# Weight conversion 512 columns at a time, norms' roots by Newton steps on VectorE, and the second attention beside the first part of the first mixing

## The chip, the cores and the metric

The kernel runs on one core of one Trainium2 chip. The metric is the device time of one execution in microseconds (us). Executions of the kernel before agreed within 0.5% on each chip that was used.

## The reference

Inputs are `q`, `k`, `v` of shape (8 batches, 12 heads, 448 rows, 64 columns) in fp32, the gains `g_q` and `g_k`, and four weight matrices that `setup_inputs` makes in float64 (a float32 array times a numpy float64 scalar stays 64-bit here). Cut to what matters:

```python
def rmsnorm(x, g):
    return x / np.sqrt(np.mean(x * x, axis=-1, keepdims=True) + 1e-06) * g
q_n, k_n = rmsnorm(q, g_q), rmsnorm(k, g_k)
attn = softmax(scale * q_n @ k_n^T)                  # per batch and head
x = (attn @ v), heads side by side                   # (8, 448, 768)
h = np.maximum(x^T @ w_tok1, 0) @ w_tok2             # mixing of rows, 448 -> 256 -> 448
u = x + h^T
return u + np.maximum(u @ w_ch1, 0) @ w_ch2          # mixing of columns, 768 -> 1536 -> 768
```

There are eight attentions and eight mixings, one each per batch.

## The kernel before

TensorE does the column mixing as block products with seven products in place of eight, for which its weights are needed as four blocks and four sums of blocks. So each weight tile is a **stage**: 128 partitions, 512 columns in, eight blocks of 128 out. A stage is converted from the two 32-bit halves of each 64-bit number: VectorE masks the exponent and the high mantissa bits, ScalarE turns both into floats, VectorE puts in the low half and the sign, and GpSimd multiplies mantissa by exponent. 36 stages are converted in this way, stored to DRAM, and reloaded for every batch as **units** of 384 KB.

```python
WCOLS = 256                         # a stage is two items of 256 columns

def convert_first(i):               # item i
    nc.vector.tensor_scalar(e_t[0:rows, 0:n], hi, 0x7FF00000, None, ALU.bitwise_and)      # L201
    nc.vector.tensor_scalar(m_t[0:rows, 0:n], hi, 0x000FFFFF, None, ALU.bitwise_and)      # L202

def convert_second(i):              # ScalarE, one item later
    nc.scalar.activation(out=e, in_=e, func=AF.Relu, bias=expo_c[0:rows, 0:1], scale=8.0)
    nc.scalar.activation(out=m.bitcast(F32), in_=m, func=AF.Identity, bias=one_c[0:rows, 0:1], scale=2.0**-20)

def convert_last(i):                # two items later
    nc.vector.scalar_tensor_tensor(out=mf, in0=lo, scalar=2.0**-52, in1=mf, op0=ALU.mult, op1=ALU.add)              # L227
    nc.vector.scalar_tensor_tensor(out=e, in0=hi, scalar=0x80000000, in1=e, op0=ALU.bitwise_and, op1=ALU.bitwise_or) # L229
    nc.gpsimd.tensor_tensor(out=dst, in0=fold(mf), in1=fold(ef), op=ALU.mult)             # L231, "the product"
    if at >= 0 and at % 2 == 1:     # the second half of a stage
        combine(at // 2)

def combine(j):                     # the stage's sums
    nc.vector.tensor_tensor(out=q[:, 4], in0=q[:, 1], in1=q[:, 3], op=ALU.add)            # L178, waits for the product
    nc.vector.tensor_tensor(out=q[:, 6], in0=q[:, 1], in1=q[:, 0], op=ALU.subtract)       # L179
    nc.gpsimd.tensor_tensor(out=q[:, 5], in0=q[:, 4], in1=q[:, 0], op=ALU.subtract)       # L180
    nc.gpsimd.tensor_tensor(out=q[:, 7], in0=q[:, 2], in1=q[:, 5], op=ALU.subtract)       # L181
    nc.sync.dma_start(out=to.rearrange("q p n -> p q n"), in_=q[:])

def one(i):                         # one item, in the order of issue
    convert_first(i); convert_second(i - 1); convert_last(i - 2); weight_load(i + 2)
```

The norm of a pair of heads (ScalarE squares, VectorE adds up, GpSimd takes the power -0.5), and the order of the whole:

```python
nc.vector.tensor_reduce(out=ms[...], in_=sq[...], axis=AX_X, op=ALU.add)                  # L749
nc.vector.tensor_scalar(ms[0:R, w], ms[0:R, w], 1.0 / D, 1e-6, ALU.mult, ALU.add)         # L753, 16 columns
nc.gpsimd.tensor_tensor(out=rs[0:R, w], in0=ms[0:R, w], in1=..., op=ALU.pow)              # L754
...
BEFORE = len(first) + 4 * KC + 3
for _, fn in merge(att_items(0, AHEAD * per + 2), weight_items(0, BEFORE)):               # attention 0
    fn()
for b in range(B):
    early, late = mlp_items(b)       # mixing b: its first part, its second layer
    if b == 0:
        then = len(first) + 2 * stage_end[3] + 2
        early = merge(early, weight_items(BEFORE, then))
        late = merge(late[:14], weight_items(then, len(chunks) + 2)) + late[14:]
    att = att_items(lo, lo + per) if b + AHEAD < B else []      # attention b + 1
    for _, fn in merge(att, early + late):
        fn()
```

## Time and profile before

| | before |
|---|---|
| median, range of 3 runs | 1572.7 us, 1570.44 to 1574.23 |
| TensorE busy over the span | 1422.2 us, 90% |
| first 403.5 us (attentions 0 and 1, all conversions, mixing 0) | "the ramp" below is the part to the last stage's store, 22.0 to 369.6 us |
| each later batch | 174.5 us, TensorE busy for 172.4 |

The prediction, further down, shows the slices, the stretches and VectorE's waits in the ramp. One more view of it will be needed: VectorE's groups of instructions in the ramp, 22.0 to 369.6 us. The columns are line, engine, operation, tiles, shapes and count; then busy us and mean ns of one; then idle time just before them, and what ended it.

```profile
L227 DVE SCALAR_TENSOR_TENSOR m_t<-raw,m_t 128x256 f32<-128x256 uint32 (+1 forms) x80 | 36.8, 460 | 9.1 <-ACT m_t L213 9.1
L229 DVE SCALAR_TENSOR_TENSOR e_t<-raw,e_t 128x256 uint32<-128x256 uint32 (+1 forms) x80 | 35.7, 446 | 0.0
L202 DVE TENSOR_SCALAR m_t<-raw 128x256 uint32<-128x256 uint32 (+1 forms) x78 | 33.5, 429 | 0.0
L201 DVE TENSOR_SCALAR e_t<-raw 128x256 uint32<-128x256 uint32 (+1 forms) x78 | 31.8, 408 | 8.7 <-DMA raw<-in_moe_w_ch_dram 8.7
...
L753 DVE TENSOR_SCALAR ms<-ms 112x16 f32<-112x16 f32 x12 | 15.2, 1268 | 0.4
```

The means are the thing to look at. Left alone, the masks L201 and L202 take 0.28 us and L227 and L229 take 0.41; in the ramp they average 0.41 to 0.46. L753 takes 0.17 left alone and averages 1.27. In order of time one sees who holds them (start, duration, engine, instruction, all in us):

```profile
311.35 1.30 POOL L562 TENSOR_TENSOR hb<-hb 128x448 f32<-128x448 f32 x1
...
311.59 1.34 DVE L229 SCALAR_TENSOR_TENSOR e_t<-raw,e_t 128x256 uint32<-128x256 uint32 x1
312.86 0.28 DVE L201 TENSOR_SCALAR e_t<-raw 128x256 uint32<-128x256 uint32 x1
...
313.01 0.72 POOL L231 TENSOR_TENSOR stage<-m_t,e_t 128x256 f32<-128x256 f32 x1 [0.36 <-DVE e_t L229]
313.06 0.82 DVE L202 TENSOR_SCALAR m_t<-raw 128x256 uint32<-128x256 uint32 x1
```

L229 starts while GpSimd's L562 runs and is not done before it has ended (311.35 + 1.30 = 312.65), at three times its free duration. L202 meets the product of the item before. Such time counts as VectorE's busy time in the page, not as a wait. **Held time** below is worked out so: for each conversion instruction of the ramp that took over 0.06 us more than its free duration, the excess, summed.

### The profile page before, as it was taken

The page shows a single profiled execution, that of the slowest core. Times are in us where ns is not written, and L with a number is a line of the kernel's source. Part 1 is how long each engine was busy: PE and PEld are TensorE (multiplying, and loading weights), DVE is VectorE, ACT ScalarE, POOL GpSimd, SP SyncE. Part 2 cuts the span into 40 slices and gives each one's busy share as a digit, 9 for nine tenths or more (in the row PEclk, how much of TensorE's full clock was granted, in tenths as well). Part 3 has the DMA queues.
Part 4 walks back from the last instruction along what each step waited for, and adds up shares of the span by engine and source line. Part 5 has one row for each costly group of instructions (what it writes and reads, how often), then busy time and mean ns, then how long its engine had stood idle before and what let it go on. Part 6 is the DMA issues. An engine that isn't in the chain of part 4 may idle for free.

```text
span 1571.7 us, 19052 instructions
## 1 busy us (share of the span) xinstructions
PE 1422.2 (90%) x6976; PEld 1054.9 (67%) x6976; DVE 662.5 (42%) x1183; ACT 511.1 (33%) x930; POOL 612.6 (39%) x514
## 2 busy tenths in 40 slices
PE   5765866497999999999999999999999999999997
PEld 2222454375577866887577766788588767787897
DVE  5765866743344233432434234433343225322321
ACT  6553444332333233322333233323333242312110
POOL 5674566644235324333235224352334234320231
PEclk9786997798999999999999999999999999999999
DMA  5456667476244552455244542555254433444353
GB/s 125 117 146 192 185 205 216 145 227 188 79 136 129 155 144 68 145 147 154 61 140 133 161 119 79 156 147 156 54 149 136 149 103 98 136 127 126 111 171 108
DMA packets 229802, 217.10 MB, mean 138 GB/s; under 512 B 98180, under 2 KB 185988, under 8 KB 229700
## 3 DMA queue, kind: packets, MB, share of 16 engines
q1 hardware_dynamic: 206178, 204.55, 44.5%
q10 hardware_dynamic: 23522, 11.24, 2.7%
q8 instruction: 58, 0.95, 0.2%
q14 instruction: 44, 0.36, 0.1%
HBM read 185.86 MB, written 29.88 MB: 137 GB/s over the span
## 4 chain that ended last, share of the span: by engine, by line
PE 76%; DVE 8%; POOL 6%; DMA 3%; issue 3%; ACT 2%; ACTq 1%; SPq 0%; POOLq 0%; DVEq 0%
PE m_ps L581 24%; PE m_ps L523 22%; PE s_ps L289 8%; PE o_ps L346 8%; PE m_ps L445 5%; PE m_ps L453 4%; PE d_ps L360 2%; POOL rs L754 2%; DMA raw<-in_moe_w_ch_dram 2%; POOL stage L231 2%; PE t_ps L424 2%; PE t_ps L274 2%; DVE m_t L202 1%; DVE m_t L227 1%; DVE e_t L229 1%
## 5 line engine op out<-in xcount | busy, mean ns | idle before, releaser
L581 PE MATMUL m_ps<-hb,unit 128*128 128x224 f32 x2016 | 402.0, 357 | 31.4 <-DMA unit<-ws 31.4
L581 PEld LDWEIGHTS m_ps<-hb,unit 128*128 128x128 f32 x2016 | 378.5, 192 | 53.7 <-issue 26.5
L295 ACT ACTIVATE e<-s_ps,rs 112x448 f32<-112x448 f32 x384 | 212.0, 633 | 190.4 <-PE s_ps L289 190.3
L523 PE MATMUL m_ps<-tu,unit 128*128 128x224 f32 x1152 | 232.9, 356 | 4.3 <-DVE r L528 4.3
L523 PEld LDWEIGHTS m_ps<-tu,unit 128*128 128x128 f32 x1152 | 217.6, 192 | 14.8 <-issue 8.5
L289 PE MATMUL s_ps<-qkT 64*112 64x448 f32 x768 | 181.6, 594 | 25.6 <-ACT qkT L276 25.6
L754 POOL TENSOR_TENSOR rs<-ms,mhalf_c 112x16 f32<-112x16 f32 (+1 forms) x49 | 148.6, 3033 | 103.2 <-DVE ms L753 94.3
L523 PE MATMUL m_ps<-uT,unit 128*128 128x224 f32 x864 | 179.4, 360 | 3.3 <-DVE r L528 3.3
L523 PEld LDWEIGHTS m_ps<-uT,unit 128*128 128x128 f32 x864 | 163.5, 193 | 22.6 <-issue 13.7
L346 PE MATMUL o_ps<-e,vt 112*64 112x448 f32 x768 | 170.0, 565 | 2.4 <-DVE uT L378 2.4
L590 POOL TENSOR_TENSOR uT<-uT,r 128x448 f32<-128x448 f32 (+1 forms) x64 | 58.7, 928 | 283.9 <-DVE r L590 168.0
L332 POOL TENSOR_TENSOR es<-e 112x896 f32<-112x896 f32 x48 | 100.1, 2085 | 125.2 <-PE d_ps L360 125.2
L289 PEld LDWEIGHTS s_ps<-qkT 64*112 64x112 f32 x768 | 65.8, 183 | 103.6 <-issue 65.9
L276 ACT ACTIVATE qkT<-t_ps,g_t 128x448 f32<-128x448 f32 x96 | 58.0, 630 | 211.4 <-PE t_ps L274 207.3
L346 PEld LDWEIGHTS o_ps<-e,vt 112*64 112x64 f32 x768 | 47.8, 139 | 117.0 <-issue 101.6
L445 PE MATMUL m_ps<-x,w_sb 112*128 112x384 f32 x256 | 94.2, 519 | 30.2 <-DVE x L430 17.9
L590 DVE TENSOR_TENSOR uT<-uT,m_ps 128x448 f32<-128x448 f32 (+1 forms) x80 | 38.8, 502 | 195.3 <-PE m_ps L581 160.5
L336 DVE TENSOR_TENSOR es<-es,e 112x896 f32<-112x896 f32 x96 | 115.2, 1200 | 11.2 <-ACT e L295 6.6
L372 DVE STREAM_TRANSPOSE dt<-d_ps 128x448 f32<-128x448 f32 x48 | 31.1, 649 | 189.4 <-PE d_ps L360 189.2
L528 DVE TENSOR_TENSOR r<-m_ps,r 128x448 f32<-128x448 f32 x72 | 44.9, 623 | 137.8 <-PE m_ps L523 94.1
L528 POOL TENSOR_TENSOR hb<-r,r 128x448 f32<-128x448 f32 x24 | 29.3, 1221 | 187.3 <-ACT r L544 187.3
L231 POOL TENSOR_TENSOR stage<-m_t,e_t 128x256 f32<-128x256 f32 x72 | 56.0, 779 | 101.2 <-DVE e_t L229 99.0
(65 smaller groups left out, 1379.8 us busy)
## 6 DMA issues: line engine op xcount, KB each, us to landing
unit<-ws SPq DMA_DIRECT2D x336, 384.0 KB, 3.3
raw<-in_moe_w_ch_dram SPq DMA_DIRECT2D x72, 256.0 KB, 3.4
ws<-stage SPq DMA_DIRECT2D x36, 512.0 KB, 3.5
vt<-in_v_dram SPq DMA_DIRECT2D x48, 224.0 KB, 2.6
out_dram<-y ACTq DMA_DIRECT2D x48, 224.0 KB, 3.3
qk<-in_q_dram SPq DMA_DIRECT2D x92, 112.0 KB, 3.5
qk<-in_k_dram SPq DMA_DIRECT2D x92, 112.0 KB, 3.3
raw<-in_moe_w_tok_dram SPq DMA_DIRECT2D x4, 224.0 KB, 3.7
```

What stands on the lines that cost most here:

```text
L231: nc.gpsimd.tensor_tensor(out=dst, in0=fold(mf), in1=fold(ef), op=ALU.mult)
L289: nc.tensor.matmul(out=ps[0:R, 0:S], lhsT=qkT[a * D:(a + 1) * D, 1, kc * R:(kc + 1) * R], rhs=qkT[a * D:(a + 1) * D, 0, :], start=True, st ...
L295: nc.scalar.activation(out=e[0:R, a, i, :], in_=pss[a][0:R, 0:S], func=AF.Exp, scale=st["rs", p][0:R, r:r + 1])
L332: nc.gpsimd.tensor_tensor(out=es[0:R], in0=e[0:R, :, 0, :], in1=e[0:R, :, 1, :], op=ALU.add)
L336: nc.vector.tensor_tensor(out=es[0:R], in0=es[0:R], in1=e[0:R, :, i, :], op=ALU.add)
L346: nc.tensor.matmul(out=o[a * D:(a + 1) * D, 0:S], lhsT=vt[0:R, a, kc * D:(kc + 1) * D], rhs=e[0:R, a, i, :], start=(kc == 0), stop=(kc == ...
L445: nc.tensor.matmul(out=ps[:, 0:HC], lhsT=w1_sb[0:R, c, jc * P:(jc + 1) * P], rhs=st["x", h][0:R, c, :], start=(c == 0), stop=(c == NS - 1))
L523: nc.tensor.matmul(out=ps[:, j * HS:(j + 1) * HS], lhsT=w[:, t, j, :], rhs=m, start=(t == 0), stop=(t == KC - 1))
L528: add = lambda e, o, x, y: e.tensor_tensor(out=o, in0=x, in1=y, op=ALU.add)
L581: nc.tensor.matmul(out=ps[:, j * HS:(j + 1) * HS], lhsT=st["w"](j, t), rhs=hb[:, HB[what], t, :], start=(t == 0), stop=(t == KF - 1))
L590: add = lambda e, o, x, y: e.tensor_tensor(out=o, in0=x, in1=y, op=ALU.add)
L754: nc.gpsimd.tensor_tensor(out=rs[0:R, w], in0=ms[0:R, w], in1=self.mhalf_c[0:R].to_broadcast([R, (hi - lo) * n]), op=ALU.pow)
```

## The change

Three things are changed at once. A stage becomes one item of 512 columns, its conversion four VectorE instructions instead of eight, with the mantissa kept in the raw buffer; fewer buffers pay for the wider tiles. The root is taken on VectorE by a first guess in integers and three Newton steps, ten instructions of 16 columns, so that GpSimd has no power to do. And attention 1 is merged with the first part of mixing 0 only, the second layer following alone; the conversions are spread anew (`BEFORE`). The diff, cut to its core:

```diff
-    UNITS = 7
+    UNITS = 5
-    cv_pool = pool("cv_pool", 4)
+    cv_pool = pool("cv_pool", 3)
-    WCOLS = 256
+    WCOLS = 512
 ...
     def convert_first(i):
-        nc.vector.tensor_scalar(e_t[0:rows, 0:n], hi, 0x7FF00000, None, ALU.bitwise_and)
-        nc.vector.tensor_scalar(m_t[0:rows, 0:n], hi, 0x000FFFFF, None, ALU.bitwise_and)
+        nc.vector.tensor_scalar(e, hi, 0x000FFFFF, 0x00100000, ALU.bitwise_and, ALU.bitwise_or)
+        nc.vector.scalar_tensor_tensor(
+            out=lo.bitcast(F32), in0=lo, scalar=2.0**-32, in1=e, op0=ALU.mult, op1=ALU.add)
+        nc.vector.tensor_scalar(e, hi, 0x7FF00000, None, ALU.bitwise_and)
 ...
     def convert_second(i):
         nc.scalar.activation(out=e, in_=e, func=AF.Relu, bias=expo_c[0:rows, 0:1], scale=8.0)
-        nc.scalar.activation(
-            out=m.bitcast(F32), in_=m, func=AF.Identity, bias=one_c[0:rows, 0:1], scale=2.0**-20)
+        m = st["raw", i][0:rows, 0:n, 0].bitcast(F32)
+        nc.scalar.mul(m, m, 2.0**-20)
 ...
     def convert_last(i):
-            nc.vector.scalar_tensor_tensor(
-                out=mf, in0=lo, scalar=2.0**-52, in1=mf, op0=ALU.mult, op1=ALU.add)
             nc.vector.scalar_tensor_tensor(
                 out=e, in0=hi, scalar=0x80000000, in1=e, op0=ALU.bitwise_and, op1=ALU.bitwise_or)
-            nc.gpsimd.tensor_tensor(out=dst, in0=fold(mf), in1=fold(ef), op=ALU.mult)
-        at = i - len(first)
-        if at >= 0 and at % 2 == 1:
-            combine(at // 2)
+            nc.gpsimd.tensor_tensor(out=dst, in0=fold(lo.bitcast(F32)), in1=fold(e.bitcast(F32)), op=ALU.mult)
+        if i >= len(first):
+            combine(i - len(first))
 ...
-    BEFORE = len(first) + 4 * KC + 3
+    BEFORE = len(first) + 4
-            then = len(first) + 2 * stage_end[3] + 2
+            then = len(first) + stage_end[3] + 2
-        for _, fn in merge(att, early + late):
+        for _, fn in merge(att, early) + late if b == 0 else merge(att, early + late):
 ...
-            nc.gpsimd.tensor_tensor(
-                out=rs[0:R, w], in0=ms[0:R, w],
-                in1=self.mhalf_c[0:R].to_broadcast([R, (hi - lo) * n]), op=ALU.pow)
+            self.rsqrt(rs[0:R, w], ms[0:R, w])
+
+    def rsqrt(self, y, x):
+        t = self.st_pool.tile([128, 4 * self.NS], F32, name="nt")[0:y.shape[0], 0:y.shape[1]]
+        nc.vector.tensor_scalar(
+            y.bitcast(I32), x.bitcast(I32), -0.5, float(0x5F3759DF), ALU.mult, ALU.add)
+        for _ in range(3):
+            nc.vector.scalar_tensor_tensor(out=t, in0=y, scalar=-0.5, in1=y, op0=ALU.mult, op1=ALU.mult)
+            nc.vector.tensor_tensor(out=t, in0=t, in1=x, op=ALU.mult)
+            nc.vector.scalar_tensor_tensor(out=y, in0=t, scalar=1.5, in1=y, op0=ALU.add, op1=ALU.mult)
```

More of the change, by code (lines that the diff above doesn't have):

```diff
@@ L119, in weight_chunks @@
         w1v = moe_w_tok1.rearrange("(p c) n -> p c n", c=NS)
-        for c in range(NS):
-            for o in range(0, DT, WCOLS):
-                n = min(WCOLS, DT - o)
-                first.append((R, w1v[:, c, o:o + n], w1_sb[0:R, c, o:o + n], None))
+        for c in range(0, NS, 2):
+            first.append((R, [w1v[:, c:c + 2, :].rearrange("p c n -> p (c n)")], w1_sb[0:R, c:c + 2, :].rearrange("p c n -> p (c n)"), None))
         for j in range(NJ):
-            for o in range(0, S, WCOLS):
-                n = min(WCOLS, S - o)
-                dst = w2_sb[:, j, :, o // NS:(o + n) // NS].rearrange("p c r -> p r c")
-                first.append((P, moe_w_tok2[j * P:(j + 1) * P, o:o + n], dst, NS))
+            dst = w2_sb[:, j].rearrange("p c r -> p r c")
+            first.append((P, [moe_w_tok2[j * P:(j + 1) * P, :]], dst, NS))
         for w, group, m, t in stages:
-            rows, cols = (DC if w is moe_w_ch2 else C) // 2, w.shape[1] // 2
-            for k in range(2):
-                r = k * rows + t * P
-                src = w[r:r + P].rearrange("p (i n) -> p i n", i=2)[:, :, m * P:(m + 1) * P]
-                second.append((P, src, None, None))
+            rows = (DC if w is moe_w_ch2 else C) // 2
+            src = [w[r:r + P].rearrange("p (i n) -> p i n", i=2)[:, :, m * P:(m + 1) * P]
+                   for r in (t * P, rows + t * P)]
+            second.append((P, src, None, None))
         return first, second
@@ L143, in stage_list, with columns @@
         return l
+    def columns(i):
+        return WCOLS if chunks[i][2] is None else chunks[i][1][0].shape[-1]
     def weight_load(i):
-        rows, src, dst, split = chunks[i]
-        n = WCOLS if dst is None else src.shape[-1]
-        if src.dtype == I64:
-            t = raw_pool.tile([P, WCOLS, 2], U32, name="raw")
-            to = t[0:rows, 0:n, :]
-            if dst is None:
-                to, src = to.rearrange("p (i n) w -> p i (n w)", i=2), src.bitcast(U32)
-            else:
-                to, src = to.rearrange("p n w -> p (n w)"), src.bitcast(U32)
-        else:
-            t = raw_pool.tile([P, WCOLS], F32, name="raw")
-            to = t[0:rows, 0:n]
-            if dst is None:
+        rows, srcs, dst, split = chunks[i]
+        n = columns(i) // len(srcs)
+        wide = srcs[0].dtype == I64
+        t = raw_pool.tile([P, WCOLS, 2] if wide else [P, WCOLS], U32 if wide else F32, name="raw")
+        for k, src in enumerate(srcs):
+            to = t[0:rows, k * n:(k + 1) * n]
+            if wide:
+                src = src.bitcast(U32)
+                to = to.rearrange("p (i n) w -> p i (n w)", i=2) if dst is None else to.rearrange("p n w -> p (n w)")
+            elif dst is None:
                 to = to.rearrange("p (i n) -> p i n", i=2)
-        nc.sync.dma_start(out=to, in_=src)
+            nc.sync.dma_start(out=to, in_=src)
         st["raw", i] = t
-    def chunk_out(i):
-        rows, src, dst, split = chunks[i]
-        if dst is not None:
-            return rows, src.shape[-1], dst, split
-        at = i - len(first)
-        if at % 2 == 0:
-            st["stage"] = stage_pool.tile([P, NQ, P], F32, name="stage")
-        k = at % 2
-        return P, WCOLS, st["stage"][:, 2 * k:2 * k + 2, :].rearrange("p q n -> p (q n)"), None
     def combine(j):
@@ L191, in convert_first @@
     def convert_first(i):
-        rows, src, dst, split = chunks[i]
-        if src.dtype != I64:
+        if chunks[i][1][0].dtype != I64:
             return
-        n = WCOLS if dst is None else src.shape[-1]
-        hi = st["raw", i][0:rows, 0:n, 1]
-        e_t = cv_pool.tile([P, WCOLS], U32, name="e_t")
-        m_t = cv_pool.tile([P, WCOLS], U32, name="m_t")
-        st["cv", i] = e_t, m_t
-        nc.vector.tensor_scalar(e_t[0:rows, 0:n], hi, 0x7FF00000, None, ALU.bitwise_and)
-        nc.vector.tensor_scalar(m_t[0:rows, 0:n], hi, 0x000FFFFF, None, ALU.bitwise_and)
+        rows, n = chunks[i][0], columns(i)
@@ L204, in convert_second @@
+        lo, hi = (st["raw", i][0:rows, 0:n, w] for w in range(2))
+        e = cv_pool.tile([P, WCOLS], U32, name="e_t")[0:rows, 0:n]
+        nc.vector.tensor_scalar(e, hi, 0x000FFFFF, 0x00100000, ALU.bitwise_and, ALU.bitwise_or)
+        nc.vector.scalar_tensor_tensor(
+            out=lo.bitcast(F32), in0=lo, scalar=2.0**-32, in1=e, op0=ALU.mult, op1=ALU.add)
+        nc.vector.tensor_scalar(e, hi, 0x7FF00000, None, ALU.bitwise_and)
+        st["cv", i] = e
     def convert_second(i):
-        rows, src, dst, split = chunks[i]
@@ L206, in convert_second @@
-        if src.dtype != I64:
+        if chunks[i][1][0].dtype != I64:
             return
-        n = WCOLS if dst is None else src.shape[-1]
-        e_t, m_t = st["cv", i]
-        e, m = e_t[0:rows, 0:n], m_t[0:rows, 0:n]
+        rows, n, e = chunks[i][0], columns(i), st["cv", i]
         nc.scalar.activation(out=e, in_=e, func=AF.Relu, bias=expo_c[0:rows, 0:1], scale=8.0)
-        nc.scalar.activation(
-            out=m.bitcast(F32), in_=m, func=AF.Identity, bias=one_c[0:rows, 0:1], scale=2.0**-20)
+        m = st["raw", i][0:rows, 0:n, 0].bitcast(F32)
@@ L216, in convert_last @@
+        nc.scalar.mul(m, m, 2.0**-20)
     def convert_last(i):
-        rows, n, dst, split = chunk_out(i)
+        rows, srcs, dst, split = chunks[i]
+        n = columns(i)
+        if dst is None:
+            st["stage"] = stage_pool.tile([P, NQ, P], F32, name="stage")
+            dst = st["stage"][:, 0:4, :].rearrange("p q n -> p (q n)")
         fold = (lambda a: a.rearrange("p (r c) -> p r c", c=split)) if split else (lambda a: a)
         t = st.pop(("raw", i))
-        if chunks[i][1].dtype != I64:
+        if srcs[0].dtype != I64:
@@ L221, in convert_last @@
             nc.gpsimd.tensor_copy(out=dst, in_=fold(t[0:rows, 0:n]))
         else:
-            e_t, m_t = st.pop(("cv", i))
-            lo, hi = t[0:rows, 0:n, 0], t[0:rows, 0:n, 1]
-            e, m = e_t[0:rows, 0:n], m_t[0:rows, 0:n]
-            ef, mf = e.bitcast(F32), m.bitcast(F32)
-            nc.vector.scalar_tensor_tensor(
-                out=mf, in0=lo, scalar=2.0**-52, in1=mf, op0=ALU.mult, op1=ALU.add)
+            lo, hi = (t[0:rows, 0:n, w] for w in range(2))
+            e = st.pop(("cv", i))
@@ L229, in convert_last @@
             nc.vector.scalar_tensor_tensor(
                 out=e, in0=hi, scalar=0x80000000, in1=e, op0=ALU.bitwise_and, op1=ALU.bitwise_or)
-            nc.gpsimd.tensor_tensor(out=dst, in0=fold(mf), in1=fold(ef), op=ALU.mult)
-        at = i - len(first)
-        if at >= 0 and at % 2 == 1:
-            combine(at // 2)
+            nc.gpsimd.tensor_tensor(out=dst, in0=fold(lo.bitcast(F32)), in1=fold(e.bitcast(F32)), op=ALU.mult)
+        if i >= len(first):
+            combine(i - len(first))
@@ L707, in __init__ @@
                     out=self.g_t[a * D:(a + 1) * D, i:i + 1], in_=g.rearrange("(p o) -> p o", o=1))
-        self.mhalf_c = const.tile([P, 1], F32, name="mhalf_c")
-        nc.gpsimd.memset(self.mhalf_c[:], -0.5)
         self.ident = const.tile([P, P], F32, name="ident")
@@ L753, in norm_pair @@
             nc.vector.tensor_scalar(ms[0:R, w], ms[0:R, w], 1.0 / D, 1e-6, ALU.mult, ALU.add)
-            nc.gpsimd.tensor_tensor(
-                out=rs[0:R, w], in0=ms[0:R, w],
-                in1=self.mhalf_c[0:R].to_broadcast([R, (hi - lo) * n]), op=ALU.pow)
+            self.rsqrt(rs[0:R, w], ms[0:R, w])
+    def rsqrt(self, y, x):
+        nc = self.nc
+        t = self.st_pool.tile([128, 4 * self.NS], F32, name="nt")[0:y.shape[0], 0:y.shape[1]]
[5 more added lines that the diff above has]
+            nc.vector.scalar_tensor_tensor(out=y, in0=t, scalar=1.5, in1=y, op0=ALU.add, op1=ALU.mult)
 @with_exitstack
```

## The prediction

> **What bounds the kernel now.** I read the page's slices first, then the busy time of each engine in stretches that I cut at the borders of the phases, then VectorE's waits in the first phase, then its order of time. On the page, these lines show a slow start and a saturated rest:
>
> ```profile
> PE   5765866497999999999999999999999999999997
> DVE  5765866743344233432434234433343225322321
> PEclk9786997798999999999999999999999999999999
> ```
>
> Each digit is a fortieth of the span (39.3 us). PE is at 40 to 80% in the first ten slices (to about 400 us) and at 90% or more after. The stretches say it in numbers (columns: us, then busy us and count of PE, PEld, DVE, ACT, POOL, then granted clock, DMA share, GB/s):
>
> ```profile
> 22.00:369.60 347.60, 241.24 (x1020) 144.46 (x1016) 238.32 (x527) 156.29 (x313) 206.03 (x211) 0.83 0.59 173
> 369.60:403.50 33.90, 26.26 (x144) 22.94 (x144) 7.67 (x14) 8.65 (x15) 8.54 (x7) 0.90 0.70 218
> 403.50:578.00 174.50, 172.38 (x872) 129.47 (x872) 65.34 (x98) 55.23 (x96) 62.77 (x44) 1.00 0.44 127
> ```
>
> A later batch takes 174.50 us and PE is busy for 172.38 of them, so nothing that the change does can save more than 2.1 us there; six such batches and a last one of 121.7 us follow 403.5 us. All the room lies in the first 403.5 us, where the weights are converted beside attentions 0 and 1 and the first mixing. Which engine sets the pace there? VectorE's waits between 22.0 and 369.6 us (who waited for whom: us in total, times, longest):
>
> ```profile
> DVE stage L178 <- POOL stage L231: 66.0, 36, 5.7
> DVE dt L372 <- PE d_ps L360: 21.7, 6, 8.8
> DVE m_t L227 <- ACT m_t L213: 9.1, 1, 9.1
> DVE e_t L201 <- DMA raw<-in_moe_w_ch_dram: 8.7, 9, 3.2
> DVE ms L749 <- ACT sq L746: 3.0, 1, 3.0
> ```
>
> They sum to 108.5 us; with 238.3 us busy that is 346.8 of 347.6. So VectorE's program, busy or held by another engine, is the whole length of the ramp, though it is only 69% busy. Any item of the change must be weighed as time put into or taken out of this queue. The largest item, 66.0 us, is 36 waits (one per stage of 512 columns) for GpSimd's product of mantissa and exponent. In order of time they have two sizes:
>
> ```profile
> 288.95 3.75 POOL L754 TENSOR_TENSOR rs<-ms,mhalf_c 112x16 f32<-112x16 f32 x1
> 292.78 1.04 POOL L265 TENSOR_TENSOR qk<-qk,rs 112x512 f32<-112x512 f32 x1
> 293.78 0.72 POOL L231 TENSOR_TENSOR stage<-m_t,e_t 128x256 f32<-128x256 f32 x1
> ...
> 294.54 0.29 DVE L178 TENSOR_TENSOR stage<-stage 128x128 f32<-128x128 f32 x1 [4.60 <-POOL stage L231]
> 300.95 0.29 DVE L178 TENSOR_TENSOR stage<-stage 128x128 f32<-128x128 f32 x1 [0.83 <-POOL stage L231]
> ```
>
> 0.84 us is the product itself (0.73) and its handover; 4.60 is the same wait behind a power (3.75) and a scaling (1.04). Of the 36, nine stand behind a power (4.60 six times; 3.71; 2.30; 5.70): 39.3 us, 31.7 over nine times 0.84.
>
> **What the Trainium skill says.**
> - "VectorE: DVE Perf Modes", section "Mode 2×_2P": an fp32 operation with one SBUF source can do two elements a cycle, one with two tensor sources cannot. The trace agrees: the 256-column masks (L201, L202) start 0.20 us apart, the two-input ones (L227, L229) 0.33 apart.
> - The same page, "The TRN2 errata", puts a fixed cost on each SBUF instruction and advises 512 elements or more. The trace: 0.35 us for 192 columns of L227, 0.41 for 256, so about 1.0 ns a column and 0.15 us fixed; but independent instructions start about 0.08 us before the former ends, so half of that is hidden already.
> - "SBUF — State Buffer", "Who interferes with whom": VectorE instructions of those two kinds and GpSimd block each other for a whole instruction. The trace agrees: the 16-column L753 takes 0.175 us in the median and up to 1.77 where GpSimd's es sum runs.
> - "GPSIMD Engine Reference", "Performance pitfalls": reads whose byte step is over 8 are slow. The new product reads the raw words at exactly 8; no run yet shows that it stays fast.
>
> **The change part by part**, as time in VectorE's queue of the ramp.
> 1. **Wide conversion, VectorE's own time: 0.** Before, a stage has 8 instructions: twice (0.20+0.20+0.33+0.35) and 0.41 for the two sums, 2.57 us. After, 4: a mask of 512 columns is 0.28+256 x 0.47 ns = 0.40, a two-input one 0.41+256 x 1.04 ns = 0.68. The second reads what the first wrote and the third overwrites what the second read; dependent neighbours (L372 to L374) start 0.03 after the former's end. So 0.43+0.72+0.32+0.69+0.41 = 2.57. The halved count is eaten by the new dependence.
> 2. **Wide product: +19 us.** VectorE waits for the second half only, 0.84; after, for all of it. 192 columns take 0.60 on GpSimd and 256 take 0.73: 2.0 ns a column, so 512 take 1.24, with handover 1.36. 36 x 0.52 = 19.
> 3. **Power off GpSimd: -32 us**, the 31.7 above.
> 4. **Newton on VectorE: +25 us.** Ten dependent instructions of 16 columns; an 8-column one takes 0.166 us, and the three small ones at the start (0.21 each) follow 0.25 apart. I take 0.20, so 2.0 us a norm, 12 to 13 norms in the ramp.
> 5. **Scaling right after Newton: +5 us.** It ran in the power's shadow while VectorE was held; now it locks the shared port (1.04 us) against the next masks, 13 times, perhaps half not hidden.
> 6. **Weights' DMA: -6 us.** Loads stay two items ahead, but an item is now a whole stage (7 to 8 us, not 4) against 3.4 us from issue to landing; most of the 8.7 goes. The raw buffer is freed later, by GpSimd, so not all.
> 7. **ScalarE: -10 us.** 256 columns take 0.50 us and 192 take 0.45, so 512 take about 0.70: a stage costs 1.4 instead of 2.0, and exponentials stand less behind conversions; I take half of the 21.7 us that VectorE waited for the denominator. The 9.1 stays: ScalarE is held by PE's first second-layer product, which waits for stored weights as before.
> 8. **Second attention ahead of the second layer: -6 us.** It moves VectorE's work, it does not remove it. 28 stages instead of 23.5 and all twelve attention steps now stand beside the first part. But after the last stage is stored (369.6), 33.9 us followed with one attention step in them; after: 3.2 us to land, 2.9 to load, 16 us for 42 matmuls of 0.38 and some 5 of transposes, about 27.5.
> 9. **Five unit buffers instead of seven: 0.** A 384 KB unit lands 3.3 us after issue and feeds six matmuls, 2.27 us. Four units ahead are 9.1 us of cover; in the second layer, where two are held at once, about 3 us. PE shows no DMA wait after 403.5 us.
> 10. **Start: -1 us.** Only one half's root (2.0 us), not both powers (3.3), stands before the first scaling.
>
> Sum: 0+19-32+25+5-6-10-6+0-1 = -6 us. The later batches get 2.0 us of Newton per pair on a VectorE that is 37% busy, and lose the powers on a GpSimd that is 36% busy: 0. So 1572.7-6 = **1567 us**.
>
> **Rivals.**
> - **The ramp really shrinks by 30 to 40 us** (about 1535). For it: GpSimd loses 12 x 3.4 us of power in a phase where it is 59% busy, handovers halve, and the chain of waits has the power's line at 7.9% of the first 404 us. It needs contention and the 21.7 us to vanish with the power. Against it: Newton puts 25 us back on the engine that is the queue, and the wider product 19.
> - **VectorE becomes worse and the ramp grows** (about 1590 to 1600). Each of Newton's nine two-input steps can be held by a GpSimd instruction, as L753 was; at 0.3 us a step that is 13 us more, and a strided product at a slower rate would add 36 times that. Against it: in program order GpSimd's next work after the sum es is the scaling, which waits for Newton.
> - **Later batches starve on five buffers** (2 us a batch, about 1582). The queue's loads of q and k wait for PE up to 22 us and block units behind them. Against it: the first attention work after such a wait gives PE 3.4 us without units.
>
> **Range and chances.** The sum's uncertain terms are items 2, 5, 7 and contention, each 5 to 10 us; together about 17 us either way. A little more room is on both sides for the rivals: 1543 to 1590. Two per cent is 31 us; that needs nearly all of the first rival: 0.13. Slower by as much needs two others together: 0.05. Within: 0.82.
>
> **What would show it.** In the new profile VectorE's busy and held time should again fill the ramp, and the batch after it begin near 397 us. The waits for the product should be 1.3 to 1.4 us each, with no group of 4.6. Newton's instructions should average 0.2 us. A later batch should stay at 174.5 us with no DMA wait on PE. I am wrong on the ramp if those waits fall well under 50 us in sum or VectorE is no longer the queue; wrong on buffers if PE's digits drop after 400 us; wrong on the lock if Newton's mean is over 0.3 us.

## The result

The changed kernel is correct and takes 1551.33 us in the median of 4 runs (1550.73 to 1552.22), against 1572.49 for the kernel before (4 runs). The ratio is 0.9866, with a 95% interval from 0.9849 to 0.9883. A ratio here is always the mean time of one kernel's fast runs over that of the other's of the same rounds, so it is not quite the ratio of the medians. The time lies in the predicted range, and the class is the one that got the largest chance (within 2%), though the gain of 21 us is more than three times the 6 us that were predicted.

The slices of the page after:

```profile
PE   5778668477999999999999999999999999999998
DVE  6977777751454435543454435543454435422321
PEclk9989877789999999999999999999999999999999
```

PE's low digits are still the first ten slices (of 38.8 us now), and VectorE's are higher in every later batch, by Newton's steps (60 of them, 15.0 us in a batch), without any effect on PE's nines. The stretches that answer to those of before, cut at the last stage's store and at the start of batch 1 (us, then busy us and count of PE, PEld, DVE, ACT, POOL, clock, DMA share, GB/s):

```profile
22.00:353.30 331.30, 237.23 (x1037) 145.57 (x1036) 249.92 (x503) 139.42 (x238) 161.15 (x160) 0.86 0.63 181
353.30:383.48 30.18, 22.40 (x121) 21.29 (x121) 4.58 (x10) 4.44 (x8) 2.60 (x4) 0.89 0.70 211
383.48:557.98 174.50, 172.41 (x873) 129.51 (x873) 81.22 (x158) 55.34 (x96) 46.90 (x38) 1.00 0.44 126
```

The ramp is 16.3 us shorter (347.6 to 331.3), the stretch between the last store and batch 1 is 3.7 us shorter, a later batch is the same to the hundredth, and the rest of the difference between the two profiled spans (1571.7 to 1550.2) is 1.4 us in the last batch. VectorE's waits in the ramp:

```profile
DVE stage L162 <- POOL stage L212: 51.9, 36, 1.5
DVE uT L570 <- PE m_ps L561: 11.1, 2, 10.3
DVE dt L352 <- PE d_ps L340: 5.3, 4, 1.9
DVE ms L728 <- ACT sq L725: 2.9, 1, 2.9
```

The waits for the product are 36 equal ones of 1.44 us now. With 249.9 us busy these lists sum to 321.1; most of the other 10 us are the gaps between dependent instructions, of which Newton's have the most. VectorE's groups in the ramp, those that answer to the ones of before:

```profile
L183 DVE SCALAR_TENSOR_TENSOR raw<-raw,e_t 128x512 f32<-128x512 uint32 (+2 forms) x39 | 37.9, 971 | 1.3
...
L210 DVE SCALAR_TENSOR_TENSOR e_t<-raw,e_t 128x512 uint32<-128x512 uint32 (+2 forms) x40 | 30.4, 759 | 0.0
L185 DVE TENSOR_SCALAR e_t<-raw 128x512 uint32<-128x512 uint32 (+2 forms) x40 | 22.8, 571 | 1.4
L182 DVE TENSOR_SCALAR e_t<-raw 128x512 uint32<-128x512 uint32 (+2 forms) x39 | 22.8, 584 | 0.0
...
L732 DVE TENSOR_SCALAR ms<-ms 112x16 f32<-112x16 f32 x13 | 6.8, 525 | 0.4
```

Free durations are 0.43 us for L182 and L185 and 0.69 for L183 and L210. And one norm in order of time:

```profile
293.04 2.09 POOL L312 TENSOR_TENSOR es<-e 112x896 f32<-112x896 f32 x1
...
293.38 1.78 DVE L732 TENSOR_SCALAR ms<-ms 112x16 f32<-112x16 f32 x1
...
295.20 0.17 DVE L739 TENSOR_SCALAR rs<-ms 112x16 int32<-112x16 int32 x1
295.41 0.18 DVE L742 SCALAR_TENSOR_TENSOR nt<-rs 112x16 f32<-112x16 f32 x1
...
297.40 1.09 POOL L245 TENSOR_TENSOR qk<-qk,rs 112x512 f32<-112x512 f32 x1 [2.27 <-DVE rs L744]
297.63 1.49 DVE L183 SCALAR_TENSOR_TENSOR raw<-raw,e_t 128x512 f32<-128x512 uint32 x1
```

Newton's ten instructions take 0.175 us each and start 0.21 apart, 2.1 us a norm. The scaling follows at once, and the conversion instruction beside it (L183) takes 1.49 us instead of 0.69: that is item 5 of the prediction, to be seen by eye.

**VectorE's ledger of the ramp**, in us:

| | before | after | difference |
|---|---|---|---|
| length | 347.6 | 331.3 | -16.3 |
| busy | 238.3 | 249.9 | +11.6 |
| of it: conversion (instructions on the raw tiles) | 118.6 | 109.7 | -8.9 |
| of it: Newton's ten instructions | 0 | 22.7 | +22.7 |
| of it: the norm's small instruction (L753, L732) | 15.2 | 6.8 | -8.4 |
| wait for GpSimd's product | 66.0 | 51.9 | -14.1 |
| wait for the softmax's denominator on PE | 21.7 | 5.3 | -16.4 |
| wait for the weights' DMA | 8.7 | 0 | -8.7 |
| wait for ScalarE or PE at the second layer's start | 9.7 | 11.1 | +1.4 |
| the rest: the wait for the squares and gaps between instructions | 3.2 | 13.1 | +9.9 |

The length is the busy time and the four waits and the rest together. Such a sum closes for any engine, so it does not show that VectorE sets the pace; the experiments have to.

### The profile page after: what moved, and what is told of

It reads as the page before. It is cut to its first block, busy times and chain, and to the rows that moved or that the text cites. A ratio compares the mean times of both kernels' runs of the same rounds, so it can differ in the third digit from the quotient of the medians.

```text
span 1550.2 us, 19250 instructions
## 1 busy us (share of the span) xinstructions
PE 1415.5 (91%) x6976; PEld 1054.6 (68%) x6976; DVE 761.6 (49%) x1513; ACT 491.9 (32%) x850; POOL 468.1 (30%) x424
## 4 chain that ended last, share of the span: by engine, by line
PE 76%; DVE 12%; POOL 3%; issue 3%; ACT 2%; DMA 1%; ACTq 1%; POOLq 0%; SPq 0%; DVEq 0%
PE m_ps L561 24%; PE m_ps L503 22%; PE o_ps L326 8%; PE s_ps L269 8%; PE m_ps L425 5%; PE m_ps L433 4%; POOL stage L212 3%; PE d_ps L340 2%; PE t_ps L404 2%; DVE raw L183 2%; PE t_ps L254 2%; DVE e_t L210 2%; DVE es L316 1%; DVE e_t L182 1%; DVE ms L728 1%
## 5 line engine op out<-in xcount | busy, mean ns | idle before, releaser
L561 PE MATMUL m_ps<-hb,unit 128*128 128x224 f32 x2016 | 402.1, 357 | 30.2 <-DMA unit<-ws 30.2
L503 PE MATMUL m_ps<-tu,unit 128*128 128x224 f32 x1152 | 238.0, 361 | 12.7 <-DVE hb L508 12.7
L503 PEld LDWEIGHTS m_ps<-tu,unit 128*128 128x128 f32 x1152 | 220.8, 195 | 26.9 <-DVE hb L508 13.1
L503 PEld LDWEIGHTS m_ps<-uT,unit 128*128 128x128 f32 x864 | 161.7, 191 | 26.2 <-issue 11.6
L326 PE MATMUL o_ps<-e,vt 112*64 112x448 f32 x768 | 166.0, 553 | 1.8 <-DVE uT L358 1.8
L312 POOL TENSOR_TENSOR es<-e 112x896 f32<-112x896 f32 x48 | 100.7, 2098 | 136.3 <-PE d_ps L340 136.3
L316 DVE TENSOR_TENSOR es<-es,e 112x896 f32<-112x896 f32 x96 | 127.8, 1331 | 4.9 <-DVE es L316 0.5
L570 DVE TENSOR_TENSOR uT<-uT,m_ps 128x448 f32<-128x448 f32 (+1 forms) x80 | 38.8, 502 | 167.6 <-PE m_ps L561 155.3
L245 POOL TENSOR_TENSOR qk<-qk,rs 112x512 f32<-112x512 f32 x46 | 55.3, 1203 | 197.3 <-ACT e L275 95.0
L728 DVE TENSOR_REDUCE ms<-sq 112x16 f32<-112x1024 f32 (+1 forms) x49 | 58.3, 1191 | 62.4 <-ACT sq L725 62.4
L509 ACT ACTIVATE hb<-hb 128x448 f32<-128x448 f32 x72 | 41.5, 577 | 149.1 <-DVE hb L508 117.4
```

The costliest lines, as they stand in the source:

```text
L312: nc.gpsimd.tensor_tensor(out=es[0:R], in0=e[0:R, :, 0, :], in1=e[0:R, :, 1, :], op=ALU.add)
L316: nc.vector.tensor_tensor(out=es[0:R], in0=es[0:R], in1=e[0:R, :, i, :], op=ALU.add)
L326: nc.tensor.matmul(out=o[a * D:(a + 1) * D, 0:S], lhsT=vt[0:R, a, kc * D:(kc + 1) * D], rhs=e[0:R, a, i, :], start=(kc == 0), stop=(kc == ...
L503: nc.tensor.matmul(out=ps[:, j * HS:(j + 1) * HS], lhsT=w[:, t, j, :], rhs=m, start=(t == 0), stop=(t == KC - 1))
L561: nc.tensor.matmul(out=ps[:, j * HS:(j + 1) * HS], lhsT=st["w"](j, t), rhs=hb[:, HB[what], t, :], start=(t == 0), stop=(t == KF - 1))
L570: add = lambda e, o, x, y: e.tensor_tensor(out=o, in0=x, in1=y, op=ALU.add)
```

## The experiments

Each changes one thing of the kernel before or after. All were correct, with 5 rounds each; "before" was 1572.2 to 1574.7 us in the median of the four chips that were used. Two theories stood at first. One was the prediction's sum: the power's removal, Newton, the wide product and the order give and take what was worked out, and some item is a little off. The rival was that one removed thing gives much more than its visible wait: the power on GpSimd, which may have caused the waits for the denominator and the long small instructions as well, or the narrow conversion.

### One part at a time

Newton alone. The kernel before with this edit:

```diff
-            nc.gpsimd.tensor_tensor(out=rs[0:R, w], in0=ms[0:R, w], in1=..., op=ALU.pow)
+            self.rsqrt(rs[0:R, w], ms[0:R, w])
```

> The kernel before with the roots by Newton steps on VectorE and nothing else. Theory A (VectorE's queue is the ramp; the prediction's items 3 to 5): 31.7 us of waits behind the power go, about 26 us of Newton and a few us of scaling come, so -5 to +3 us against before. Theory B (the power also delayed GpSimd's es sum, which then held VectorE's small norm instruction, and delayed q and k, which held the denominator): these go too, L753's mean falls from 1.27 us to under 0.6 in the ramp and the waits for the denominator from 21.7 us to under 10, so -12 to -20 us.

Measured: 1578.31 us, ratio 1.0022 (1.0009 to 1.0035): 3.5 us slower, at the upper end of theory A (-5 to +3) and far from theory B. The waits for the product fell by 25.3 us (66.0 to 40.7) and VectorE's busy time rose by 25.0 (238.3 to 263.3), with some 7 us of gaps between Newton's dependent steps. The small instruction still averaged 1.19 us and the waits for the denominator 19.4 in sum. So the power had caused neither, and the rival falls as far as it goes by the power. Taking the power off GpSimd pays on this queue just about what Newton costs.

The order alone:

```diff
-        for _, fn in merge(att, early + late):
+        for _, fn in merge(att, early) + late if b == 0 else merge(att, early + late):
```

> The kernel before with the second attention beside the first part of the first mixing only. Theory A: the attention's work moves ahead in VectorE's queue and none leaves it; only the end after the last stored stage loses its attention step, so -3 to -6 us. Rival: the second layer's part of the ramp, freed of attention, runs at PE's pace, -15 us or more; or the first part, loaded with twelve instead of eight attention steps, stalls more, +5 us or more.

Measured: 1566.86 us, ratio 0.9952 (0.9939 to 0.9965). Batch 1 starts 8.7 us earlier than in the kernel before. The waits for the denominator fell from 21.7 to 11.0, those for the product rose from 66.0 to 76.9. It is a gain of 8 us, near the 6 us of item 8, but only half of it is the stretch after the last store (33.9 to 29.9 us), of which item 8 spoke; the other half is in the ramp.

The width alone, that is the changed kernel with the power and the old order put back. It is a bundle: 512 columns, the new arithmetic with the mantissa kept in the raw buffer, one conversion buffer and two unit buffers fewer, and two stages instead of six and a half beside attention 0. The place of the stages and VectorE's instruction count are taken apart below; the new arithmetic and the buffers were not tried at 256 columns.

```diff
 (against the changed kernel)
-            self.rsqrt(rs[0:R, w], ms[0:R, w])
+            nc.gpsimd.tensor_tensor(out=rs[0:R, w], in0=ms[0:R, w], in1=..., op=ALU.pow)
-        for _, fn in merge(att, early) + late if b == 0 else merge(att, early + late):
+        for _, fn in merge(att, early + late):
```

> The kernel before with 512-column conversion (and the five unit buffers that make room for it), the power still on GpSimd, the old order. Theory A: product waits +19 us, DMA waits -6, ScalarE -10, with the power's waits unchanged: 0 to +8 us against before. Rival (half as many handovers is the gain): -10 us or more.

Measured: 1542.61 us, ratio 0.9802 (0.9788 to 0.9817). This one part gains some 31 us, where theory A had a loss of 0 to 8 us, and is **faster than the whole change**. So the rival holds, by the narrow conversion. VectorE's groups in its ramp (22.0 to 341.4 us):

```profile
L183 DVE SCALAR_TENSOR_TENSOR raw<-raw,e_t 128x512 f32<-128x512 uint32 (+2 forms) x39 | 33.3, 853 | 1.3
...
L734 DVE TENSOR_SCALAR ms<-ms 112x16 f32<-112x16 f32 x12 | 5.8, 484 | 0.4
```

The length went from 347.6 to 319.4, by 28.2. Busy time fell by 30.4: the conversion from 118.6 to 99.5 and the small instruction from 15.2 to 5.8. The waits for the product are 68.8 us in sum, hardly more than before, though each is longer. The waits for the denominator are 25.0, not fewer; the runs on the place of the conversions, below, come back to them. The held time of the conversion, worked out as said above, is 28.0 us in 59 instructions before and 15.4 in 29 here. Put down to the GpSimd instruction beside it, 5.8 of it lay before beside the product and 7.8 beside GpSimd's two stage sums; here none beside the product and some 4 beside the sums. That leaves 90.6 us of own time before (118.6 - 28.0) and 84.1 here (99.5 - 15.4). Against these 6.5 us stand 2.6 us of new gaps, which busy time leaves out: L183 and L185 wait for what stands just before them. As for the small instruction, 10 of 12 were held beside GpSimd's sum es before (L332), and 3 of 12 are here (L312): that sum, of 2.09 us, has mostly ended by then (it often starts 3.3 us before the small instruction, where 0.4 was usual). Why is not settled.

### The parts together

Width and Newton without the order (the changed kernel, with the one line of the order undone):

> The changed kernel with the old order of the second attention. If the order gives its -4 us independently of the rest, this is 4 us slower than the changed kernel, about 1555 us; if the order is what gave most of the 21 us, it is 1562 us or more.

Measured: 1556.77 us, ratio 0.9883 (0.9867 to 0.9898). Against the width alone, on the same chip, Newton costs 14 us here, not 3.5. Busy time rose by 32.1 us (207.9 to 240.0), the waits for the product fell by only 16.8 (68.8 to 52.0). The floor of those waits is 36 x 1.44, some 52 us: beyond it stood only some 17 us in the wide version. In the version before, 66.0 - 36 x 0.84 = 35.8 stood beyond the floor, of which Newton alone took 25.3. So a third of what the power's removal gave by itself was gone once the width was there. The order of time of the width alone shows how:

```profile
221.63 3.01 POOL L735 TENSOR_TENSOR rs<-ms,mhalf_c 112x16 f32<-112x16 f32 x1
...
227.05 0.29 DVE L162 TENSOR_TENSOR stage<-stage 128x128 f32<-128x128 f32 x1 [3.38 <-POOL stage L212]
```

The usual wait behind a power is 3.4 us here and was 4.6 before (the prediction shows one at 288.95). VectorE's four wide instructions keep it at work until 2.04 us after the power's start, where the four narrow ones had ended after 0.99, and the power takes 3.01 us, not 3.75. Newton also puts more in than it did alone: the conversion's busy time rises by 9.1 us (99.5 to 108.6), where it rose by 1.6 in the narrow version (118.6 to 120.2); seven wide instructions are held by the scaling, for 5.0 us.

Width and order without Newton (the changed kernel, with the power put back):

> The changed kernel with the power back on GpSimd (wide conversion and the new order stay). If Newton costs the changed kernel what it cost beside the wide conversion alone (14 us, 1556.8 against 1542.6), this is about 1538 us and the best so far. If the new order is only of use with Newton (in the order alone, waits behind the power grew from 66.0 to 76.9 us), it is 1548 us or more.

Measured: 1538.16 us, ratio 0.9776 (0.9760 to 0.9791): again faster than the whole change. The table of the parts, as ratio to before, and the start of batch 1 in the profile:

| | power | Newton |
|---|---|---|
| narrow, old order | 1, 403.5 us | 1.0022, 407.9 us |
| narrow, new order | 0.9952, 394.8 us | not run |
| wide, old order | 0.9802, 373.7 us | 0.9883, 389.4 us |
| wide, new order | 0.9776, 370.3 us | 0.9866, 383.5 us |

The width gives all of the gain; read by the start of batch 1, the order gives 3 to 9 us and Newton takes 4 to 16 us back.

### Is it the width, or where the conversions stand?

The wide kernel also does fewer stages beside attention 0. So the narrow kernel got fewer early ones, and the wide kernel more.

```diff
 (against the kernel before)
-    BEFORE = len(first) + 4 * KC + 3
+    BEFORE = len(first) + 6
```

> The kernel before, 256 columns at a time, with two stages instead of six and a half converted beside the first attention, as the wide version has it; nothing else. If the 32 us that the wide conversion gave alone come from this move (fewer products that stand behind a power), most of it is here: -20 us or more. If they come from half as many instructions that meet GpSimd on the shared port, this is -8 to +8 us.

Measured: 1572.67 us, ratio 0.9999 (0.9983 to 1.0015): no difference beyond the noise of some 2.5 us.

```diff
 (against the width alone)
-    BEFORE = len(first) + 4
+    BEFORE = len(first) + 2 * KC + 2
```

> The wide conversion alone (power on GpSimd, old order) with six stages beside the first attention, as the kernel before has it. The mirror of the run with few early: if width gives the gain, about 1540 to 1548 us; if the move does, 1560 us or more.

Measured: 1546.61 us, ratio 0.9829 (0.9814 to 0.9845). Some 4 us of the 31 hang on the place; the rest comes with the width.

These two runs also set right a comparison that was drawn above. One of VectorE's waits in the ramp of the wide kernel with many early stages is

```profile
DVE dt L352 <- PE d_ps L340: 10.6, 6, 4.7
```

The waits for the denominator hang on the place: with two early stages they are 31.6 us in the narrow kernel and 25.0 in the wide one, with six or six and a half 21.7 and 10.6. At equal place the width lowers them by 7 to 11 us, about what item 7 had forecast. But one or two long waits make up most of each sum (15.0 us of the 31.6, 8.8 of the 21.7), and no run separates ScalarE's shorter work from the rest of the width.

### How much of the width is VectorE's instruction count?

The width alone, with each of VectorE's four instructions issued as two halves; loads, ScalarE and the product stay wide.

```diff
 (one of the four)
-            nc.vector.scalar_tensor_tensor(out=e, in0=hi, scalar=0x80000000, in1=e, ...)
+            for o in (0, n // 2):
+                m = n // 2
+                nc.vector.scalar_tensor_tensor(
+                    out=e[:, o:o + m], in0=hi[:, o:o + m], scalar=0x80000000, in1=e[:, o:o + m], ...)
```

> The wide version alone (1542.6 us, VectorE 99.5 us busy on the conversion in the ramp), with each of VectorE's four conversion instructions of a stage issued as two halves of 256 columns; loads, ScalarE's two instructions and GpSimd's product stay 512 wide. Theory of meetings on the shared port: each instruction can be held by one of GpSimd's, so with eight instructions a stage VectorE's busy time on the conversion goes back to about 115 to 119 us (before: 118.6) and the norm's small instruction back to over 1 us in the mean; the ramp gives back 15 to 25 us, time 1558 to 1568. Rival, the gain of the width lies in the rest (fewer handovers, ScalarE's wider instructions, the whole product asked for at once): busy on the conversion stays under 106 us and the time within 5 us of 1542.6. A result between says how much is VectorE's share.

Measured: 1553.0 us, ratio 0.9873 (0.9856 to 0.9891), which neither text expected: the time lies between the two, and the busy time on the conversion (105.4 us) on the rival's side. The split gives back a third of the width's gain (some 11 us of 31), and little of that is VectorE's own: of the 5.9 us more on the conversion, 3.6 are own time and 2.3 held, and the ramp's gaps fall by 2.5 us, since the halves do not wait for each other. In that, item 1 of the prediction was right: the halved count is worth some 1 us by itself. The ramp's waits for the product rose by 7.0 (68.8 to 75.8), and GpSimd's groups account for them. First the halves, then the width alone (columns as for VectorE's groups):

```profile
L744 POOL TENSOR_TENSOR rs<-ms,mhalf_c 112x16 f32<-112x16 f32 x12 | 46.0, 3832 | 11.0 <-DVE ms L743 10.6
```

```profile
L735 POOL TENSOR_TENSOR rs<-ms,mhalf_c 112x16 f32<-112x16 f32 x12 | 38.9, 3241 | 11.0 <-DVE ms L734 10.5
```

GpSimd's power takes 0.59 us longer in the mean, 7.1 in sum, when VectorE's conversion is in halves. Holding goes both ways, and VectorE pays for it in its wait for the product behind the power. The mean mixes two sizes; four of the twelve are like this one:

```profile
228.15 4.83 POOL L744 TENSOR_TENSOR rs<-ms,mhalf_c 112x16 f32<-112x16 f32 x1
```

A power beside an idle VectorE takes 2.90 us. What lengthens it seems to be a run of VectorE instructions without a gap: 3.01 us where the run ends 0.25 after the power's start (wide, the next instruction waits 0.03 for the one before), 3.75 where four narrow ones end 0.99 after it, 4.83 where eight halves end 2.06 after it; the steps agree (0.74 and 0.74, 1.08 and 1.07). That is read from the traces, not tested, and four powers of 2.90 beside halves do not fit. The power itself holds nothing: none of the 37 conversion instructions (35 with the width) that ran wholly beside one took over 0.05 us more than free. The small instruction stayed short (0.48 us), so its relief comes with the other part of the width: one group of instructions per stage and one product, for which VectorE stands idle, in place of two groups of which the second runs beside the first one's product. That this arrangement accounts for the other two thirds is what remains by subtraction and what the held times of the width alone suggest; no run isolates it.

### Do the waits for the product end the ramp one for one?

The changed kernel, with a stage's sums issued one item later, so that VectorE asks for the product a whole item after it was issued:

```diff
         def one(i):
-            # combine(i - 2) at the end of convert_last(i - 2)
+            if i - 3 >= len(first):
+                combine(i - 3 - len(first))
             if 2 <= i < len(chunks) + 2:
                 convert_last(i - 2)
```

> The changed kernel with the sums of a stage (the two VectorE instructions that wait for GpSimd's product) put one item later, after the next chunk's first three instructions; nothing else. If VectorE's queue is the ramp, the 51.9 us of waits for the product go and the time falls by 35 to 50 us, to 1501 to 1516. Rival: the ramp is as long as the chain conversion, store, load, PE; then the waits turn into others (DMA, denominator, PE) and it falls by 15 us or less.

Measured: 1540.09 us, ratio 0.979 (0.9773 to 0.9807), 11 us better than the changed kernel, not the 35 to 50 of the first theory. VectorE's waits in the ramp:

```profile
DVE e_t L182 <- POOL stage L213: 19.6, 13, 2.1
...
DVE stage L162 <- POOL stage L213: 1.9, 2, 1.4
```

50 us of waits went; 19.6 came back at the next stage's first mask, which needs the exponent buffer that GpSimd is still reading (three buffers). Waits for PE, the DMA and another of GpSimd's sums took some 12 more, and Newton's instructions 5.9 (0.22 us each, not 0.175), since VectorE now runs beside the product. The rival of the expectation holds. The same on the version with width, order and the power:

> The wide version with the new order and the power on GpSimd (1538.2 us), with the sums of a stage issued one item later, so that VectorE asks for GpSimd's product a whole item after it was asked for. If the waits for the product end the ramp one for one, their 68 us go and the time falls to about 1475 to 1495. If VectorE's queue only meets the next wait (a buffer of the exponents still being read by GpSimd, the denominator, PE), as in the delayed run of the changed kernel (11 us gained of 52 us of waits removed), it falls by 5 to 15 us, to 1523 to 1533. This is also the candidate for the fastest version.

Measured: 1523.44 us, ratio 0.9686 (0.9672 to 0.9699): 15 us better than without the delay; the second text holds. The wait for the exponent buffer is 30.6 us in 15 waits there. So with a fourth exponent buffer, paid for by a fourth unit buffer in place of five:

```diff
-    UNITS = 5
+    UNITS = 4
-    cv_pool = pool("cv_pool", 3)
+    cv_pool = pool("cv_pool", 4)
```

> The delayed version with the power, with four instead of three buffers for the exponents (and four instead of five weight units, which makes room for them). In the delayed run of the changed kernel, 19.6 us of VectorE's waits were for GpSimd still reading an exponent buffer. If that wait is a matter of buffers, a fourth removes it and the ramp shortens by 10 to 20 us against the same version with three; if GpSimd's own pace holds VectorE, the wait moves elsewhere and the time is within 5 us of it. The fourth unit less may cost later batches: then a batch is over 174.5 us.

Measured: **1517.17 us, ratio 0.9645 (0.9632 to 0.9658)**, the fastest of all and better than both kernels. The wait for the exponent buffer is gone from VectorE's list:

```profile
DVE dt L353 <- PE d_ps L341: 17.0, 8, 4.9
DVE uT L571 <- PE m_ps L562: 13.3, 3, 10.7
DVE r L509 <- POOL r L509: 6.0, 2, 3.9
```

But of 30.6 us removed only 6.3 came off the time, between the two texts: busy time rose from 219.5 to 237.9 us in a ramp of 296, 8.4 of it on the conversion. From batch 1 to the end it takes 1166.6 us, as the changed kernel does (1166.7), so four unit buffers cost nothing either.

### Is it Newton's own time?

The changed kernel with two steps in place of three:

```diff
-        for _ in range(3):
+        for _ in range(2):
```

> The changed kernel with two Newton steps instead of three (a slightly less exact root, allowed here if the comparison passes). It removes three dependent VectorE instructions of some 0.21 us per norm, 12 to 13 norms in the ramp, plus two or so instructions a norm's share of meetings on the shared port: if Newton's own time in VectorE's queue is what costs (theory A), the ramp shortens by 8 to 10 us and the time is 1541 to 1544. If Newton costs by something else (the order of work, GpSimd's freed slots), the time stays within 3 us of 1551.

Measured: 1541.82 us, ratio 0.9805 (0.9792 to 0.9819), still correct, 9.5 us better. 13 norms x 3 instructions x 0.21 us are 8.2 us in the ramp. So what Newton puts into VectorE's queue there comes out at the end about one for one, although VectorE is only some 75% busy. This run, and not the ledger, supports VectorE's queue as what sets the pace in the ramp; the delayed runs limit it, since waits taken out of the same queue came back in part elsewhere.

## Why the prediction was right, and where it was not

The frame held in part: a later batch stays at 174.5 us, all but 1.4 us is moved in the first 400 us, and work put into VectorE's queue there counts about one for one (two Newton steps). A wait taken out of it does not: of 50 us, 11 came off the time. Of the signs that were named, the product's waits (1.44 us each, hardly over the 1.3 to 1.4, none of 4.6, 51.9 in sum), Newton's mean and the later batches came true; batch 1 did not begin near 397 us but at 383.5.

That the time lies in the range is in good part luck. The items of the width (1, 2, 6, 7 and 9) sum to a loss of 3 us, and the width gained 31; those of the root (3, 4, 5 and 10) sum to a gain of 3, and Newton beside the width cost 13 to 14; the order was put at 6 and gave some 3 to 5 as the last part. An error of 34 us was half cancelled by one of 16.

- **Item 1 failed, and is the largest error.** "The halved count is eaten by the new dependence" is nearly true of own time (90.6 us to 84.1, with 2.6 us of new gaps, so some -4, not 0). What it left out is the held time: the width alone takes 12.6 us of it off the conversion and 9.4 off the norm's small instruction. The prediction had quoted the small instruction at up to 1.77 us, but looked on holding only as a risk of Newton's, never as a cost of the eight narrow instructions to be removed.
- **Items 2 and 3 were right in size and wrong as a sum of independent terms.** The longer wait is 36 x (1.44 - 0.84) = 21.6 us against 19 (the product took 1.29 us, not 1.24, so its reads at a step of 8 bytes stayed fast), and together with it the net of -14.1 leaves -35.7, against -32. But in the wide version the power's removal took only 16.8 us of waits away. The width had earned the rest by itself, and Newton's side of the bargain, worth +4 us by itself, is +14 beside the width. Newton should have been set against what the other parts leave.
- **Item 4 was near**: 13 x 2.1 = 27 us against 25; the run with two steps shows that one step of the three is felt in full. The second rival's fear that Newton's steps would be held did not come true in the ramp: 0.175 us each (0.25 in a later batch, where the length stayed the same).
- **Item 5 was right**: nine conversion instructions of the changed kernel's ramp are held by the scaling, for 5.8 us.
- **Item 6 was near**: -8.7 us of DMA waits for -6.
- **Item 7 is not settled.** ScalarE's two instructions became as short as forecast (0.72 and 0.66 us, 1.4 a stage), and the waits for the denominator fell by 16.4. But the width alone has 25.0 us of them, the order alone 11.0, and the width with six early stages 10.6: place, order and width all move them, and what ScalarE's part is stays open.
- **Item 8 was near**: 8 us alone, 3 to 6 beside the other parts. The stretch after the last store is 30.2 us, not 27.5.
- **Item 9 was right**, even for four buffers. **Item 10** can't be seen apart.
- **The first rival** (a ramp shorter by 30 to 40 us) was described as a gift of the power's departure. Batch 1 starts 20 us earlier in the changed kernel, which has no power, and 30 us earlier with the width alone, which keeps it. Its size was nearly real, its cause was not the power.
- **One reading is off, and nothing rests on it**: after 403.5 us come five batches of 174.5, one of 167.6 and one of 128.2 us, not six of 174.5 and one of 121.7.

Left open: why GpSimd's sum es comes earlier in the wide version, whether it is the gaps in VectorE's work that let the power through, and how the other two thirds of the width's gain divide between fewer groups, one product and fewer DMA waits (8.7 to 1.8 us).

## What to carry to other kernels

When two engines share a port, look at the mean duration of an engine's instructions against their free duration before weighing a change: time in which one engine holds another is booked as busy time and shows up in no list of waits. A part that moves work off a wait onto the bounding queue should be weighed beside the other parts, not alone, since both may count on the same wait. Removing a wait from the engine that sets the pace, even all 50 us of it, gave back a fifth to a third here, because the engine met the next buffer and the other engine's port.

## What the Trainium skill lacked or had wrong

- "VectorE: DVE Perf Modes", "The TRN2 errata", advises 512 elements for the sake of a fixed cost per instruction. The width gained 31 us, but VectorE's own time was only some 4 us of that (6.5 less, with 2.6 of new gaps) over some 160 instructions fewer; the larger part was time held by GpSimd (12.6 us on the conversion, 9.4 on the small instruction) and other waits. The page does not connect the advice with holding.
- "SBUF — State Buffer", "Who interferes with whom": that the first to issue has the shared pair for its whole instruction is borne out for GpSimd's sums: a VectorE instruction of 0.17 us took up to 1.78 beside one of 2.09, and averaged over the ramp 1.27 before and 0.48 with the width. It is not for GpSimd's power: beside 3 to 4.83 us of it VectorE's conversion instructions kept their free duration, while the power itself went from 3.24 to 3.83 us in the mean when VectorE issued eight conversion instructions instead of four.
- No page gives the duration of a power on GpSimd against Newton steps on VectorE: for 112 x 16 elements 2.9 us beside an idle VectorE and up to 4.83 beside a busy one, against ten dependent instructions 0.21 us apart.
